# Eight routed experts on one core: turning the gathered tokens by DMA transposes of 16-bit planes instead of on TensorE

## The chip, the cores and the metric

One core of a Trainium2 chip. TensorE (PE) multiplies matrices and its results land in PSUM; VectorE (DVE), ScalarE (ACT) and GpSimd (POOL) work on vectors; SyncE (SP) only issues transfers here. Each engine runs its own list of instructions in order, and an instruction that waits holds up everything behind it on that engine. 16 DMA engines move data between the chip's memory (HBM) and the core's working memory (SBUF). The metric is the device time of one execution in microseconds (us).

## The reference

Attention with capped scores over 8 batches, 12 heads, 448 positions and a head dimension of 64 gives x, 3584 tokens of 768 numbers. Then a mixture of eight experts, where each expert gets exactly 448 tokens:

```python
logits = x @ w_gate                      # 3584 x 8
order = np.argsort(-logits.flatten())    # greedy, best first
for idx in order:
    tok, e = int(idx) // E, int(idx) % E
    if assigned[tok] >= 0 or counts[e] >= cap: continue   # cap = 448
    assigned[tok] = e; counts[e] += 1
for e in range(E):
    mask = assigned == e
    h = np.maximum(x[mask] @ w1[e], 0.0)   # 768 -> 1024
    out[mask] = h @ w2[e]                  # 1024 -> 768
```

All numbers are float32.

## The kernel before

**Attention** fills about the first 335 us and writes x to a DRAM tensor `xs`. It is the same in both kernels and is not needed further.

**Routing** (`Routing`). The order of assignment is found expert by expert: whichever expert fills up first is settled first, then its tokens are taken out and the next is searched. In this text the experts are numbered one to eight in that order (`p` is that number less one). A search finds a threshold by comparing a packed key of all tokens with several values at a time, over three key parts A, B, C: VectorE and ScalarE each take some of the comparisons (tiles `cmpD` and `cmpA`; each leaves a count in a column of `r_cd` or `r_ce`), then one small matmul on TensorE at line 507 adds the counts up and VectorE forms the next thresholds. `finalise`, the end of a routing, turns the threshold into a list of 448 token numbers: matmuls at lines 614, 615, 636 and 644, and last `idx`, the row numbers, on VectorE. The last expert needs no search (`last`).

**The experts** (`ffn_all`). Every float32 operand is split into a high part in TensorE's float32r form and a low remainder (`xgh`/`xgl`, `w1h`/`w1l`, `w2h`/`w2l`, two halves of `hh`), and a product is three matmuls. ScalarE makes the high parts (line 755 for weights) and GpSimd the low parts of the weights (line 759). The first layer (`ffn1`) takes 8 blocks of 18 matmuls, 128x128 by 128x448 at line 827; the second (`ffn2`) takes 8 blocks `u` of 24 or 16 matmuls, 128x128 by 128x384 at line 855. So an expert is 144 + 176 = 320 large matmuls, and this text calls them steps 1 to 320. Three PSUM buffers `psH` take the results in turn; ScalarE empties them (`hh`, `on`, `y`).

**What an expert needs first.** When the next expert's `idx` is there, GpSimd gathers its tokens from `xs` with four indirect DMAs (line 782) into the one tile `xg` (`xgp`), tokens on partitions. A matmul needs the 768 features on partitions, so x must be turned. `xtr(p,c)` does that for one chunk of 128 features: four TensorE transposes (line 798) into PSUM, then ScalarE writes `xgh` (line 803) and VectorE `xgl` (line 804). For expert two and later these chunks stand between the matmuls of the expert ahead.

**What sets the order.** Within `ffn_all` PE, ACT, DVE and POOL run in the order in which the program is written. `tick()` is called after each large matmul, counts steps in `now`, and resumes the routing, which is a generator: `yield n` asks to be resumed n steps later, and a negative number asks for an absolute step. So the routing's instructions lie between the large matmuls by step count, not by time. SP's order was left to the scheduler of the framework. The weights of the next expert are fetched by `load1` and `load2` on SP, once `ei`, the expert's number, is read (`TENSOR_LOAD ei`).

Of the kernel before, what the change touches and what calls it, by code (L numbers as in the profile page):

```python
# [7 lines left out]
AF=mybir.ActivationFunctionType; ALU=mybir.AluOpType; AX=mybir.AxisListType  # L8
# [323 lines left out]
class Routing:  # L332
# [266 lines left out]
    def finalise(s,wp,L,update):  # L599
# [49 lines left out]
        s.results.append((idx,s.ei))  # L649
        yield 1  # L650
        if update:
          with s.tc.issue_after(mark.ins) if s.cur==0 else nullcontext():
            z=wp.tile([112,1],F32,name="zz")
            v.tensor_scalar(z,oi[:,0,0,0:1],0.0,None,op0=ALU.mult)
# [14 lines left out]
    def phases0(s,wp,L,turned):  # L669
        HA=[7,10]; HB=3  # L670
        for p in range(s.E):
            s.hA=HA[min(p,len(HA))-1] if p else 7; s.hB=HB; s.na=2 if p<9 else 1
            s.cur=p
            if p:
                s.propose(L,0,s.NC)
                yield 30
            yield from (s.search(wp,turned if p==0 else ()) if p<s.E-1 else s.last(wp))
            yield -((p-1)*320+145) if p>1 else 4
            yield from s.finalise(wp,L,p<s.E-1)


W1B=4; W2B=4
def ffn_all(nc, tc, ctx, rt, xs, w1, w2, out, ident, E, wp, deferred, xctx, gen):
# [4 lines left out]
    res=rt.results  # L688
# [12 lines left out]
    ctx.enter_context(tc.manual_schedule(engines={ET.PE,ET.Activation,ET.DVE,ET.Pool}))  # L701
    with tc.issue_after(rt.mark[0].ins):
        units(1)
    posts()
    m=0
    wu=[None]; end=[-99]
# [64 lines left out]
    CP=[[int(y) if y!='-' else None for y in x] for x in ',,,,,-01,2-3,45'.split(',')]  # L771
# [5 lines left out]
    def gather(p):  # L777
        if p>=E or p in xgs: return
        need(p)
        t=xgs[p]=xgp  # L780
        for j,(o,n) in enumerate(TS):
            g=nc.gpsimd.indirect_dma_start(out=t[:n,j*DM:(j+1)*DM],out_offset=None,in_=xs,in_offset=bass.IndirectOffsetOnAxis(ap=res[p][0][:n,j:j+1],axis=0))  # L782
        return g
# [8 lines left out]
    def xtr(p,c):  # L792
        if p>=E or c is None: return
        newx(p)
        gather(p)
        ps=pt.tile([128,512],F32,name="psX")
        for j,(o,n) in enumerate(TS):
            nc.tensor.transpose(ps[:,o:o+128],xgs[p][:,j*DM+c*128:j*DM+c*128+128],ident)  # L798
        cutx(p,c,ps)
    def cutx(p,c,ps):  # L800
        h,l=xgT[p]
        src=ps[:,:C]
        nc.scalar.activation(h[:,c,:],src,AF.Copy)  # L803
        lo=nc.vector.tensor_tensor(l[:,c,:],src,h[:,c,:].bitcast(F32),op=ALU.subtract)
    pend=[]; cnt=[0]; cur=[0]; bc=[0]; BG=11
    def tick(n=1):
        cnt[0]+=n; bc[0]+=n; now[0]+=n
        if bc[0]>=BG:
            if pend: bc[0]=0; scatter(*pend.pop(0))
        if len(res)>cur[0]+1 and cur[0]+1 not in xgs: bc[0]=0; gather(cur[0]+1)  # L810
        if cnt[0]>=hint[0]:
            cnt[0]=0; step()
    hh={}
# [52 lines left out]
    need(0)  # L866
    WG=3; NW=12; WJ=4
    for i in range(WG): load1(0,i)
    mk=gather(0)
    with tc.issue_after(mk.ins):  # L870
        tok=xgp[0:1,2*DM:2*DM+1]
        for i in range(WG,W1B): load1(0,i,tok)
        load2(0,0,tok)
        load2(0,1,tok)
    warm(NW)
    step(); step()
    step()
# [5 lines left out]
    for p in range(E):  # L883
        lastp=p==E-1; cur[0]=p
        for f in range(FC):
            if f==0: load2(p,2)
            if f+W1B-1<FC and (p==0 or f+W1B-1>=W1B): load1(p,f+W1B-1) if (p,1,f+W1B-1) not in raw else None
            if f==2: load2(p,3)
            work={}
            if f+2<FC and (p,1,f+2) not in spl: work[3]=[lambda: split1(p,f+2)]  # L890
            at={0:[(11,0,0)],1:[(11,0,1)],2:[(11,0,2)],3:[(11,1,0)],4:[(11,0,3)],5:[(11,1,1)],6:[(11,1,2)],7:[(11,1,3)]}
            if p==0: at={1:[(11,0,0)],2:[(11,0,1)],3:[(11,0,2)],4:[(11,0,3)],5:[(11,1,0)],6:[(3,1,1),(11,1,2)],7:[(3,1,3)]}
            for n,hf,i in at.get(f,()): work[n]=[lambda hf=hf,i=i: split2(p,hf,i)]
            if p==1 and f==0: work[1]=[lambda: xtr(1,4)]; work[4]=[lambda: xtr(1,5)]
            ffn1(p,f,work)
        if lastp:
            while pend: scatter(*pend.pop(0))
            ih=f2.tile([128,2],I32,name="ih")
            for k in range(2): nc.gpsimd.tensor_scalar(ih[:,k:k+1],res[p][0][:,2:3],2.0,float(k),op0=ALU.mult,op1=ALU.add)
            nc.gpsimd.drain()  # L900
            lp[0]=False
            out2=out.rearrange("n (q d) -> (n q) d",q=2)
            for t,hf in [(t,hf) for t in (3,0,1,2) for hf in range(2)]:
                ffn2(p,t,hf,[])
                if t==2: put(out2,ih[:,hf:hf+1],ons[p][0][:,t*DM+hf*HD:t*DM+hf*HD+HD])
                elif hf==1: scatter(p,t)
            break
        for u in range(8):
            if u==4: load1(p+1,0); load1(p+1,1)
            if u==5: load1(p+1,2); load2(p+1,0)  # L910
            if u==6: load1(p+1,3)
            if u==7: load2(p+1,1)
            wk={5:{14:[lambda: split1(p+1,0)]},6:{8:[lambda: split1(p+1,1)]}}.get(u,{})
            if p<1 and u==7: wk={15:[lambda: xtr(1,3)]}
            ffn2(p,u%4,u//4,(CL if p<1 else CP)[u],wk)
            if u>3: pend.append((p,u%4))


def full(nc,tc,q,k,v,cap,wg,w1,w2,out):
    with ExitStack() as ctx:  # L920
# [2 lines left out]
        xs=dr.tile([3584,768],F32,name="xs")  # L923
        NDEF=4
        xd=dr.tile([2 if NDEF<4 else NDEF-2,128,6,448],F32,name="xd")
        ident=cp.tile([128,128],F32,name="ident"); make_identity(nc,ident)
        L1=cp.tile([112,32,8],F32,name="L1")
        r=Routing(nc,cp,3584,8); r.ident=ident; r.tc=tc
# [18 lines left out]
        ffn_all(nc,tc,ctx,r,xs,w1,w2,out,ident,8,wp,deferred,xctx,r.phases(wp,L1,turned))  # L947


_INS=["q","k","v","cap","moe_w_gate","moe_w1","moe_w2"]  # L950
# [24 lines left out]
```

## Time and profile before

| | |
|---|---|
| median of 3 runs | 906.47 us (906.41 to 906.98) |
| the profiled execution: its own time | 906.85 us |
| its span, first to last instruction | 905.1 us |
| granted TensorE clock, mean | 0.995 |
| ACT, DVE, POOL busy | 564.0, 604.0, 349.9 us |

The profiled execution is 1.75 us longer than its span (start and end of the program lie outside the span) and 0.38 us over the median. Busy times overlap between engines. PE's matmuls are pipelined, so the duration of one (0.34 or 0.36 us) is longer than its distance from the next; the distance between starts is what counts.

### The profile page before, as it was taken

How to read it: one execution, taken by the hardware profiler on the slowest of the kernel's cores; microseconds unless marked ns; L12 is line 12 of the kernel's file. 1: busy time of each engine (PE TensorE's matmuls, PEld its weight loads, DVE VectorE, ACT ScalarE, POOL GpSimd, SP SyncE). 2: the span in 40 equal slices, each digit the busy share in tenths (PEclk: the TensorE clock that was granted, in tenths of full speed). 3: DMA queues.
4: the chain of work that ended last, by engine and by line, in shares of the span. 5: the costliest groups of instructions: out<-in, count | busy, mean ns of one | idle time of the engine just before them, and what ended most of it. 6: DMA issues, size and time to landing. Idle time of an engine off the chain costs nothing.

```text
span 905.1 us, 17559 instructions
## 1 busy us (share of the span) xinstructions
PE 876.5 (97%) x6320; PEld 643.3 (71%) x6320; DVE 604.0 (67%) x2004; ACT 564.0 (62%) x844; POOL 349.9 (39%) x501
## 2 busy tenths in 40 slices
PE   6899999999999997799999999999999999999997
PEld 3333444444333345789989989989999999999997
DVE  3688988989888888766776776767767764231210
ACT  6998898889899948273582672762752752532521
POOL 8100000000000009482593492592682773754841
PEclk9999999999999999999999999999999999999999
DMA  8799999997994017741915616407407407416301
GB/s 117 113 136 140 128 171 173 139 164 120 198 175 72 1 58 246 248 157 45 313 45 171 196 36 226 157 19 236 150 18 253 149 3 251 149 55 236 112 10 53
DMA packets 291704, 123.09 MB, mean 136 GB/s; under 512 B 224768, under 2 KB 275712, under 8 KB 291104
## 3 DMA queue, kind: packets, MB, share of 16 engines
q1 hardware_dynamic: 285104, 99.70, 49.9%
q0 software_dynamic: 4656, 22.02, 6.8%
q8 instruction: 50, 0.82, 0.4%
q10 hardware_dynamic: 1856, 0.23, 0.2%
q14 instruction: 38, 0.31, 0.1%
HBM read 97.15 MB, written 24.77 MB: 135 GB/s over the span
## 4 chain that ended last, share of the span: by engine, by line
PE 72%; issue 12%; POOL 5%; DVE 5%; SPq 3%; DMA 1%; ACT 1%; POOLq 0%; ACTq 0%; DVEq 0%
PE psH L827 20%; PE psH L855 18%; PE psA L189 12%; PE psS L148 10%; PE psM L206 4%; SPq L92 2%; PE psS L153 2%; POOL w1l L759 2%; PE psX L798 2%; PE psM L37 1%; POOL out_dram L840 1%; POOL w2l L759 1%; DVE es L165 1%; POOL xg L782 1%; DVE cmpD L503 1%
## 5 line engine op out<-in xcount | busy, mean ns | idle before, releaser
L855 PE MATMUL psH<-w2h,hh 128*128 128x384 f32 x896 | 247.0, 342 | 0.0
L855 PE MATMUL psH<-w2l,hh 128*128 128x384 f32 x512 | 175.0, 342 | 0.0
L154 ACT ACTIVATE e<-psS 128x896 f32<-128x896 f32 x168 | 147.6, 909 | 31.3 <-PE psS L148 18.7
L855 PEld LDWEIGHTS psH<-w2h,hh 128*128 128x128 f32 x896 | 162.3, 189 | 0.2
L159 ACT ACTIVATE e<-e,bias 128x1792 f32<-128x1792 f32 (+2 forms) x74 | 147.3, 1991 | 2.0
L827 PE MATMUL psH<-xgh,w1h 128*128 128x448 f32 x384 | 143.4, 373 | 0.3 <-ACT xgh L803 0.3
L827 PE MATMUL psH<-xgh,w1l 128*128 128x448 f32 x384 | 141.6, 369 | 0.0
L827 PE MATMUL psH<-xgl,w1h 128*128 128x448 f32 x384 | 141.2, 368 | 0.0
L148 PE MATMUL psS<-tq,tk 64*64 64x448 f32 x1152 | 130.9, 548 | 7.4 <-DVE tq L133 3.4
L759 POOL TENSOR_TENSOR w1l<-w1r,w1h 128x768 fp32r<-128x768 f32 x62 | 114.2, 1843 | 28.6 <-ACT w1h L755 22.5
L189 PE MATMUL psA<-e,nv 64*64 64x448 f32 x1104 | 120.9, 541 | 1.2 <-DVE xT L199 1.2
L759 POOL TENSOR_TENSOR w2l<-w2r,w2h 128x768 fp32r<-128x768 f32 x64 | 118.1, 1846 | 9.0 <-ACT w2h L755 8.7
L459 POOL TENSOR_SCALAR r_Bt<-r_b 112x4 f16<-112x4 int32 x1 | 0.2, 199 | 303.7 <-DVE rin L243 303.7
L165 DVE TENSOR_TENSOR es<-es,e 64x896 f32<-64x896 f32 (+2 forms) x74 | 100.4, 1356 | 2.7 <-ACT e L159 1.3
L835 DVE SCALAR_TENSOR_TENSOR hh<-psH,hh 128x64 fp32r<-128x64 f32 (+1 forms) x128 | 44.1, 386 | 81.2 <-ACT hh L833 79.7
L861 ACT ACTIVATE on<-psH 128x384 f32<-128x384 f32 x48 | 23.6, 491 | 119.6 <-PE psH L855 119.6
L855 PEld LDWEIGHTS psH<-w2l,hh 128*128 128x128 f32 x512 | 96.5, 189 | 0.0
L148 PEld LDWEIGHTS psS<-tq,tk 64*64 64x64 f32 x1152 | 43.7, 133 | 73.9 <-issue 40.7
L189 PEld LDWEIGHTS psA<-e,nv 64*64 64x64 f32 x1104 | 46.5, 134 | 59.9 <-issue 50.5
L833 ACT ACTIVATE hh<-psH 128x448 fp32r<-128x448 f32 x64 | 34.8, 544 | 73.2 <-PE psH L827 61.1
L827 PEld LDWEIGHTS psH<-xgh,w1h 128*128 128x128 f32 x384 | 72.5, 189 | 5.9 <-ACT xgh L803 0.5
L827 PEld LDWEIGHTS psH<-xgh,w1l 128*128 128x128 f32 x384 | 72.3, 188 | 5.7
(334 smaller groups left out, 1320.6 us busy)
## 6 DMA issues: line engine op xcount, KB each, us to landing
w1r<-in_moe_w_dram SPq DMA_DIRECT2D x64, 384.0 KB, 3.9
w2r<-in_moe_w_dram SPq DMA_DIRECT2D x32, 768.0 KB, 8.0
k<-in_k_dram SPq DMA_DIRECT2D x92, 112.0 KB, 3.4
q<-in_q_dram SPq DMA_DIRECT2D x92, 112.0 KB, 4.0
nv<-in_v_dram SPq DMA_DIRECT2D x72, 128.0 KB, 3.9
xs<-xn SPq DMA_DIRECT2D x4, 1344.0 KB, 7.4
xs<-xn SPq DMA_DIRECT2D x4, 896.0 KB, 5.1
xd<-xT SPq DMA_DIRECT2D x2, 1344.0 KB, 7.0
```

Of the source, the lines that this page charges most:

```text
L148: for c in range(2): nc.tensor.matmul(ps[c*64:c*64+64,h,:S],tks[g,0][hp,o,u*128+c*64:u*128+c*64+64],tks[g,1][hp,o,:],start=True,stop=True)
L154: nc.scalar.activation(ev(g,r),ps[:,:,:S],AF.Tanh,scale=sr[0])
L159: act=lambda: nc.scalar.activation(e,e,AF.Exp,scale=sr[1],bias=bias)
L165: t=es_t[g]; add=lambda o,a,b: nc.vector.tensor_tensor(o,a,b,op=ALU.add)
L189: nc.tensor.matmul(avp[g,o][h*64:h*64+64,:S],lhs,rhs[hp,h,:],start=(j==0 and x==0),stop=j==3)
L206: nc.tensor.matmul(ps[g*32:g*32+32,:S],lhs,rhs,start=first,stop=last)
L759: (eng or nc.gpsimd).tensor_tensor(view(l),r,view(h).bitcast(F32),op=ALU.subtract)
L827: nc.tensor.matmul(ps[:,:C],a[:,c,:],b[:,c,:],start=(m==0),stop=(m==DC*3-1)); m+=1
L833: nc.scalar.activation(h[:,:C],ps[:,:C],AF.Relu)
L835: nc.vector.scalar_tensor_tensor(h[:,d:d+b-a],ps[:,a:b],0.0,h[:,a:b].bitcast(F32),op0=ALU.max,op1=ALU.subtract)
L855: nc.tensor.matmul(ps[:,:HD],h[:,f,a:a+128],spl[p,2,hf,f//2][w][:,f%2,:],start=(m==0),stop=(m==nm-1))
L861: if t<3: nc.scalar.activation(ons[p][0][:,t*DM+hf*HD:t*DM+hf*HD+HD],ps[:,:HD],AF.Copy)
```

## The change

1. For experts three to eight the TensorE transposes are gone. Instead, for each of the four gathered groups of tokens (128, 128, 128 and 64 rows), ScalarE copies the tile `xg` as 16-bit numbers into a tile `pl`, low halves and high halves apart (the "planes"; 1536 numbers per row, two buffers), and SP writes `pl` to a DRAM tensor `xz`. When all four are written, two DMA transposes on SP, 384 columns each, bring `xz` back turned, into the same tile `xg`, where the halves meet again as float32. Then `cutt` splits two chunks at a time (ScalarE 128x896, VectorE 128x896), at three places in block 6 of the second layer.
2. The four plane copies are placed 22, 30, 38 and 46 steps after the gather. Two of the next expert's first-layer weight loads are asked for right at the gather.
3. The end of a routing from expert three on may start at step 100 of the expert ahead (before: 145). Where the search ends later than that, it starts 4 steps after the search. So the 614/615/636/644 matmuls and the gather lie earlier.
4. SP is now also in written order. Two ordering hints around the start of the experts are dropped.

```diff
-            yield -((p-1)*320+145) if p>1 else 4
+            yield -((p-1)*320+100) if p>1 else 4
...
+    TD=22; TJ=8; xq=[]
+    def planes(p,j):
+        o,n=TS[j]
+        pl=fp.tile([128,2,DM],I16,name="pl",bufs=2)
+        nc.scalar.activation(pl[:n],xgs[p][:n,j*DM:(j+1)*DM].bitcast(I16).rearrange("p (d h) -> p h d",h=2),AF.Copy)
+        nc.sync.dma_start(xz[2*o:2*o+2*n].rearrange("(p h) d -> p h d",h=2),pl[:n])
+        if j==3:
+            for a in (0,3): nc.sync.dma_start_transpose(xgp[:,a*C:a*C+3*C].bitcast(I16).rearrange("p (c t) -> p c t",c=3),xz[:,a*128:a*128+384])
+    def cutt(p,c0,c1):
+        newx(p)
+        h,l=xgT[p]
+        x=xgp[:,c0*C:c1*C].rearrange("p (c t) -> p c t",c=c1-c0)
+        nc.scalar.activation(h[:,c0:c1,:],x,AF.Copy)
+        nc.vector.tensor_tensor(l[:,c0:c1,:],x,h[:,c0:c1,:].bitcast(F32),op=ALU.subtract)
...
-        if len(res)>cur[0]+1 and cur[0]+1 not in xgs: bc[0]=0; gather(cur[0]+1)
+        if len(res)>cur[0]+1 and cur[0]+1 not in xgs:
+            bc[0]=0; n=cur[0]+1; gather(n)
+            if n>1:
+                load1(n,0); load1(n,1)
+                xq.extend((now[0]+TD+TJ*j,lambda j=j: planes(n,j)) for j in range(4))
+        while xq and xq[0][0]<=now[0]: xq.pop(0)[1]()
...
-            if u==4: load1(p+1,0); load1(p+1,1)
+            if u==4 and p<1: load1(p+1,0); load1(p+1,1)
...
-            ffn2(p,u%4,u//4,(CL if p<1 else CP)[u],wk)
+            if p and not lastp:
+                for m,c in {6:[(4,0),(12,2),(20,4)]}.get(u,()): wk[m]=wk.get(m,[])+[lambda c=c: cutt(p+1,c,c+2)]
+            ffn2(p,u%4,u//4,CL[u] if p<1 else [],wk)
```

The order on **ScalarE** in the second layer of expert four, while expert five is made ready, before. `hh` is the last result of the first layer, `on` and `y` empty the second layer's PSUM blocks, `cmpA` are the comparisons of the search for expert six:

```order
L833 ACTIVATE hh<-psH 128x448
L861 ACTIVATE on<-psH 128x384 x3
L500 ACTIVATE cmpA,r_cd_315<-r_VAt,r_T8A 128x252
L864 ACTIVATE y_8359<-psH 64x384
L500 ACTIVATE cmpA,r_ce_307<-r_VAt,r_H8A 128x252 x2
L861 ACTIVATE on<-psH 128x384
```

And after:

```order
L850 ACTIVATE hh<-psH 128x448
L802 ACTIVATE pl<-xg 128x1536
L878 ACTIVATE on<-psH 128x384
L802 ACTIVATE pl<-xg 128x1536 x2
L500 ACTIVATE cmpA,r_cd_316<-r_VAt,r_T8A 128x252
L802 ACTIVATE pl<-xg 64x1536
L878 ACTIVATE on<-psH 128x384
L500 ACTIVATE cmpA,r_ce_308<-r_VAt,r_H8A 128x252 x2
```

The four plane copies now stand between the PSUM blocks, and the first comparison of the next search stands behind the third of them. In the program the first copy waits for the first gather, the second for the second, the third for the third gather and for the write of the first copy's buffer to `xz`, the fourth for the last gather and the second write.

The order on **SP** from the reading of the next expert's number on, at the same place, before (`ISA` and `TENSOR_LOAD` set the address):

```order
L734 TENSOR_LOAD ei
L734 ISA x2
L743 ISA
L743 DMA w1r<-in_moe_w_dram 128x6x128
L743 ISA
L743 DMA w1r<-in_moe_w_dram 128x6x128
L743 ISA
L743 DMA w1r<-in_moe_w_dram 128x6x128
L750 ISA
L750 DMA w2r<-in_moe_w_dram 128x2x768
```

And after:

```order
L733 TENSOR_LOAD ei
L733 ISA x2
L742 ISA
L742 DMA w1r<-in_moe_w_dram 128x6x128
L742 ISA
L742 DMA w1r<-in_moe_w_dram 128x6x128
L803 DMA xz<-pl 128x1536 x3
L803 DMA xz<-pl 64x1536
L805 DMA_TRANSPOSE xg<-xz 128x3x896 x2
L742 ISA
L742 DMA w1r<-in_moe_w_dram 128x6x128
L749 ISA
```

Six rows are put in; the loads behind them keep their order, but are now queued behind the writes and the transposes, which wait for ScalarE and for the writes to land.

The order on **PE** around the last matmul of expert five's routing (line 644), before, in the second layer:

```order
L855 MATMUL psH<-w2h,hh 128x384 x2
L855 MATMUL psH<-w2l,hh 128x384
L644 LDWEIGHTS r_sel
L644 MATMUL psR<-ev,r_sel 128x28
L855 MATMUL psH<-w2h,hh 128x384 x2
```

And after, in the first layer:

```order
L844 MATMUL psH<-xgl,w1h 128x448
L844 MATMUL psH<-xgh,w1l 128x448
L644 LDWEIGHTS r_sel
L644 MATMUL psR<-ev,r_sel 128x28
L844 MATMUL psH<-xgh,w1h 128x448
```

Counted in steps, this matmul moves from behind step 183 to behind step 138 of expert four; for experts six, seven and eight likewise. For expert four it moves from 183 to 152, because its search ends later, and for expert three it stays at 188. The first line-507 matmul of the following search stands 55 steps behind the line-644 matmul in both kernels.

More of the change, by code (lines that the diff above doesn't have):

```diff
@@ L651, in finalise @@
         if update:
-          with s.tc.issue_after(mark.ins) if s.cur==0 else nullcontext():
+          if True:
             z=wp.tile([112,1],F32,name="zz")
@@ L677, in phases0, with ffn_all @@
             yield from (s.search(wp,turned if p==0 else ()) if p<s.E-1 else s.last(wp))
-            yield -((p-1)*320+145) if p>1 else 4
+            yield -((p-1)*320+100) if p>1 else 4
             yield from s.finalise(wp,L,p<s.E-1)
 W1B=4; W2B=4
-def ffn_all(nc, tc, ctx, rt, xs, w1, w2, out, ident, E, wp, deferred, xctx, gen):
+def ffn_all(nc, tc, ctx, rt, xs, xz, w1, w2, out, ident, E, wp, deferred, xctx, gen):
     C=448; DM=768; DC=6; DF=1024; FC=8; HD=384
@@ L700, in ffn_all @@
     N0=1; UN=[1,2,1,2,0,2,2,1,2,2,0,2,2,2,0,0]
-    ctx.enter_context(tc.manual_schedule(engines={ET.PE,ET.Activation,ET.DVE,ET.Pool}))
-    with tc.issue_after(rt.mark[0].ins):
-        units(1)
+    ctx.enter_context(tc.manual_schedule(engines={ET.PE,ET.Activation,ET.DVE,ET.Pool,ET.SP}))
+    units(1)
     posts()
@@ L770, in ffn_all @@
     xgs={}; xgT={}
-    CP=[[int(y) if y!='-' else None for y in x] for x in ',,,,,-01,2-3,45'.split(',')]
     CL=[[]]*6+[[None,None,0],[1,2]]
@@ L868, in ffn_all @@
     for i in range(WG): load1(0,i)
[L869 to L874, printed above, removed]
+    gather(0)
+    tok=xgp[0:1,2*DM:2*DM+1]
+    for i in range(WG,W1B): load1(0,i,tok)
+    load2(0,0,tok)
+    load2(0,1,tok)
     warm(NW)
@@ L925, in full @@
         xd=dr.tile([2 if NDEF<4 else NDEF-2,128,6,448],F32,name="xd")
+        xz=dr.tile([896,768],I16,name="xz")
         ident=cp.tile([128,128],F32,name="ident"); make_identity(nc,ident)
@@ L946, in full @@
         deferred=[lambda f=f: f((px,xr)) for f in deferred]
-        ffn_all(nc,tc,ctx,r,xs,w1,w2,out,ident,8,wp,deferred,xctx,r.phases(wp,L1,turned))
+        ffn_all(nc,tc,ctx,r,xs,xz,w1,w2,out,ident,8,wp,deferred,xctx,r.phases(wp,L1,turned))
 _INS=["q","k","v","cap","moe_w_gate","moe_w1","moe_w2"]
```

## The prediction

> **What bounds the kernel now.** The page first, then busy time by stretches over one whole expert (first layer of expert four, then its second layer).
>
> ```profile
> span 905.1 us, 17559 instructions
> PE 876.5 (97%) x6320; PEld 643.3 (71%) x6320; DVE 604.0 (67%) x2004; ACT 564.0 (62%) x844; POOL 349.9 (39%) x501
> ...
> 581.96:611.60 29.64, 29.64 (x150) 26.45 (x151) 20.59 (x104) 20.09 (x42) 26.84 (x29) 1.00 0.16 46
> 611.60:647.31 35.71, 35.71 (x223) 33.92 (x223) 26.16 (x123) 14.78 (x38) 11.32 (x12) 1.00 0.65 217
> ```
>
> PE is busy all of both stretches (35.71 of 35.71 us), at full clock. So each matmul taken out of the second layer shortens the time by its distance to the next, and each wait put in front of PE lengthens it. ScalarE is busy for only 14.78 of the 35.71 us there: room in sum, but it runs in order.
>
> The timeline of PE gives the distances.
>
> ```profile
> 621.24 0.51 PE L855 MATMUL psH<-w2h,hh 128*128 128x384 f32 x2
> ...
> 624.88 0.34 PE L855 MATMUL psH<-w2h,hh 128*128 128x384 f32 x1
> ...
> 631.81 0.34 PE L855 MATMUL psH<-w2h,hh 128*128 128x384 f32 x1
> 631.99 0.18 PE L507 MATMUL psR<-r_ce,r_bo 128*128 128x8 bf16 x1
> ...
> 632.29 0.33 PE L855 MATMUL psH<-w2l,hh 128*128 128x384 f32 x1
> ...
> 636.54 0.60 PE L798 MATMUL psX<-ident,xg 128*128 128x128 f32 x4
> 636.89 0.42 PE L855 MATMUL psH<-w2l,hh 128*128 128x384 f32 x1
> 637.15 0.52 PE L855 MATMUL psH<-w2h,hh 128*128 128x384 f32 x2
> L798 PE MATMUL psX<-ident,xg 128*128 128x128 f32 x176 | 26.4, 272 | 0.0
> ```
>
> From 621.24 to 624.88 lie 21 steps (seven triples): 0.173 us a step. A line-507 matmul makes two steps last 0.48 instead of 0.35: 0.13 us for a small matmul, somewhat less where several stand together.
>
> **The gain.** Four transposes take 636.54 to 636.89, 0.35 us, and the step behind them lasts 0.26 instead of 0.173: together 0.44 us a chunk. The group has 176 transposes, 44 chunks; two belong to expert one and six to expert two and stay. 36 x 0.44 = **15.9 us** go. ScalarE's and VectorE's splits of PSUM chunks go with them, but those waited for PE and not PE for them.
>
> **What is put in, and who waits.** Time T counts from the start of the second layer of the expert ahead (611.60 in the rows).
>
> ```profile
> 609.53 1.85 POOL L759 TENSOR_TENSOR w2l<-w2r,w2h 128x768 fp32r<-128x768 f32 x1 [1.03 <-ACT w2h L755]
> 619.02 0.19 PE L644 MATMUL psR<-ev,r_sel 128*128 128x28 f16 x1
> 619.93 0.98 POOL L782 DMA_INDIRECT xg<-xs,idx  x1 [8.55 <-DVE zz L654]
> 624.07 1.13 POOL L782 DMA_INDIRECT xg<-xs,idx  x1 [0.30 <-issue]
> 626.10 0.27 PE L477 MATMUL psR<-r_id,r_VA 112*128 112x112 f16 x2
> 626.90 0.51 ACT L500 ACTIVATE cmpA<-r_VAt,r_T8A 128x252 bf16<-128x252 f16 x1 [1.33 <-DVE r_VAt L482]
> 627.31 0.19 ACT L500 ACTIVATION_READ_ACCUMULATOR cmpA<-r_VAt,r_T8A 128x1 bf16 x1
> 628.90 0.18 PE L507 MATMUL psR<-r_cd,r_bo 128*128 128x4 bf16 x1
> ```
>
> This is the end of expert five's routing and the start of expert six's search. The first of four gathers starts 0.9 us behind the line-644 matmul, the fourth 4.1 us later. ScalarE's first comparison ran 626.90 to 627.50, 1.4 us ahead of the line-507 matmul that needs it. In the changed order that comparison stands behind the third plane copy, so three durations decide:
>
> ```profile
> DMA to landing us min/median/max: 4.4/8.0/9.2
> ...
> 614.71 1.63 SPq L743 DMA_DIRECT2D w1r<-in_moe_w_dram  x3
> 616.53 0.73 SPq L750 DMA_DIRECT2D w2r<-in_moe_w_dram  x1
> 617.51 0.37 SPq L743 DMA_DIRECT2D w1r<-in_moe_w_dram  x1
> ...
> L755 ACT ACTIVATE w1h<-w1r 128x768 fp32r<-128x768 f32 x64 | 53.5, 836 | 9.4 <-DMA w1r<-in_moe_w_dram 9.4
> L159 ACT ACTIVATE e<-e,bias 128x1792 f32<-128x1792 f32 x48 | 85.9, 1790 | 1.2
> L861 ACT ACTIVATE on<-psH 128x384 f32<-128x384 f32 x48 | 23.6, 491 | 119.6 <-PE psH L855 119.6
> ...
> w1r<-in_moe_w_dram SPq DMA_DIRECT2D x64, 384.0 KB, 3.9
> xs<-xn SPq DMA_DIRECT2D x4, 448.0 KB, 4.3
> out_dram<-on,ih POOLq DMA_INDIRECT x2, 2.6
> ```
>
> - Gather: the first row is the landing of `xg`. The median 8.0 belongs to gathers that share the engines with the loads issued just ahead of them (rows at 614.71 to 617.51). In the new SP order only two `w1r` loads lie ahead, issued as soon as `ei` is known, some 6 us ahead of the gather, and everything else is behind the writes. I take 4.4, the least; the other end is 8.0.
> - Plane copy, 1536 numbers a row: no such row. Between 0.84 (768 numbers, if 16-bit numbers went twice as fast) and 1.8 (1792). On the line through these two rows 1.5; I take that, having no reason for a faster one.
> - Write of 384 KB to `xz`: between 2.6 (the smallest indirect write) and 4.3 (448 KB to DRAM on SP). The latter is nearest in size and direction; I take 4.0.
>
> Expert five (and six alike): line 644 stands 6 first-layer steps (29.64/144 = 0.206 each) ahead of the layer's end, T = -1.2; the gather could start at -0.3, and GpSimd is done with its last weight part at 611.38, T = -0.2. First tokens 4.2; copy until 5.7; its buffer is written to DRAM by 9.7; only then the third copy, until 11.2; comparison until 11.8. PE reaches its line-507 matmul behind step 193: 49 x 0.173 plus 0.2 for the line-477 pair = 8.7. PE runs in order, so the whole second layer stands behind that matmul. **PE waits 3.1 us**, twice 6.2.
>
> Expert four, line 644 behind step 152: T = 1.8; gather 2.7, tokens 7.1, copy 8.6, write 12.6, copy 14.1, one `on` (0.5) 14.6, comparison 15.2, against step 207 at 63 x 0.173 + 0.7 for small matmuls = 11.6: **3.6**. Expert three, steps 188 and 243: 8.4, gather 9.3, tokens 13.7, 15.2, 19.2, 20.7, `y` 21.2, comparison 21.8, against 99 x 0.173 + 1.1 = 18.3: **3.5**. Experts seven and eight: no search follows, no comparison stands between the copies; the PSUM block `u`=1 is emptied at about 14, and PE needs its buffer at the start of `u`=4 (T = 15.3). **0**.
>
> The transposes: no row shows one. They move 2 x 0.69 MB as rows of 256 bytes. The nearest rows, small packets in attention (45 to 90 us), weight loads at full pace (611 to 650 us), and the smallest transfer:
>
> ```profile
> DMA packets 41729, 6.22 MB, mean 138 GB/s; under 512 B 41722, under 2 KB 41722, under 8 KB 41722
> ...
> GB/s 0 0 0 0 18 202 310 311 266 273 390 371 343 395 391 426 369 400 400 221 246 117 22 0 183 221 0 0 0 138 387 282 0 120 329 383 346 334 91 126
> ...
> wgs<-in_moe_w_gate_dram SPq DMA_DIRECT2D x6, 4.0 KB, 2.0
> ```
>
> 41729 packets in 45 us are 927 a us; one transpose has 896 x 3 = 2688 packets: 2.9 us. At 390 GB/s it is 1.8, at 138 GB/s 5.0. I take 2.9, in the packet size the nearest, and 2.0 fixed: the second lands 7.8 us behind the issue. [...]
>
> Expert five: fourth copy behind the comparison, 13.3; its write lands 17.3; second transpose 25.1; `cutt` reads it at step 292, T = 25.6 + 1.1 + 3.1 = 29.8. Covered, with 4.7 us to spare; expert four has 20.7 + 7.8 = 28.5 against 30.5. Expert three is late: fourth copy 23.3, written 27.3, second transpose 35.1, second `cutt` 36.1 (896 numbers, 0.95 on the line of the two ScalarE rows), two comparisons 37.3, against the line-507 matmul behind step 308 at 164 x 0.173 + 1.9 + 3.5 = 33.8: **3.5 more**. Its queued weight loads (384 KB and 768 KB at 390 GB/s, 3 us) then land by about 39 and are first split behind step 3 of the next expert, T above 39: just covered.
>
> Moving the end of the routing costs PE nothing by itself: the same small matmuls at 0.13. VectorE has 9 us free in the first layer (20.59 of 29.64). SP's order is otherwise the same, and the dropped hints only swap four transposes around a wait at 335 us.
>
> **Sum.** -15.9 + 6.2 + 3.6 + 3.5 + 3.5 = +0.9 us. Against the profiled execution (906.85 = span 905.1 + 1.75) 907.8; that run lies 0.4 over the median, so **907** beside 906.47: no change that can be told, since about 0.2%, 1.8 us, is what a measurement of this kernel can tell.
>
> **Rivals.** (1) *Short waits, faster.* The write lands like the smallest indirect one (2.6) or the copy runs at 0.84: with both, expert five's comparison ends at 9.1 and the waits are 0.4 + 0.4 + 0.9 + 0.8 + 0.5 = 3.0, so 894; with only one of them 899 to 902. For it: ScalarE's idle time; against: a 16-bit `cmpA` of 252 numbers takes 0.51 us, no faster than 384 float32 numbers (0.49). Waits of nothing (890.6) need the third copy to start 0.9 us behind the first; no transfer in the rows lands within that.
> (2) *Slow transposes, slower.* At 138 GB/s the second lands 12 us behind its issue; expert three loses 4.2 more and four 2.2: 914. It decides from 9.8 us on in expert four, 12.5 in five and six.
> (3) *Late gathers, slower.* If they land in 8.0 as now, every one of four waits grows by 3.6: 922. Against it: the loads that crowd them are queued behind.
> (4) *Transposes at one engine's pace.* 400 GB/s over 16 engines is 25 GB/s; 1.38 MB take 55 us, some 45 us late in each of six experts: about 1180. For it nothing but that no row shows a transpose. [...]
>
> **How the numbers follow.** The forecast, 903.5 to 911 (each write or gather 0.5 us off moves the sum by 2 to 2.5): 0.48. Rival 1: 0.25. Rival 2, with paces between: 0.13. Rival 3: 0.09. Rival 4: 0.05. Of the forecast a quarter is below 904.7, half within 0.2%, a quarter above: faster 0.25 + 0.12 = 0.37, same 0.24, slower 0.39. The range leaves out the fastest part of rival 1 and rival 4 with the worst of 2 and 3: 897 to 922.
>
> **What would show it.** Right: no line-798 group beyond 32 transposes; PE waits of about 3 us at line 507, put down to ScalarE's `cmpA` or to a DMA, once in each of experts two to five, behind steps 243, 207, 193, 193; ScalarE idle ahead of the third `pl` for `xz`; period of experts seven's and eight's preparation about 62.7 instead of 65.35 us. Wrong: no such waits (rival 1), ScalarE idle ahead of `xgh` in every expert (2, 4), ahead of the first `pl` for more than 5 us (3).

## The result, and the profile after

The changed kernel takes 947.52 us (median of 4 runs, 944.04 to 948.64) beside 906.44 for the kernel before on the same chip: ratio 1.0449 [1.0418, 1.0481], 41 us slower. Predicted were 907, range 897 to 922. One execution of the third-buffer kernel below (1221 us at a clock of 0.65) and one of the kernel before (4509 us) were disturbed and are left out.

The page, of the execution that took 944.04 us:

```profile
span 942.2 us, 17356 instructions
PE 875.3 (93%) x6176; PEld 642.3 (68%) x6176; DVE 640.8 (68%) x1986; ACT 592.6 (63%) x850; POOL 348.4 (37%) x501
```

PE does 144 matmuls fewer and is busy hardly less (875.3 beside 876.5 us) in a span that is 37.1 us longer. VectorE, with 18 instructions fewer, is busy 36.8 us longer (640.8 beside 604.0): some of its instructions must have become longer.

Where the time lies, layer by layer, from PE's timeline (first large matmul of a layer to the first of the next, us):

| layer | before | after | difference |
|---|---|---|---|
| two, second | 35.36 | 40.43 | +5.07 |
| three, first | 30.29 | 33.32 | +3.03 |
| three, second | 35.09 | 35.26 | +0.17 |
| four, first | 30.24 | 36.93 | +6.69 |
| four, second | 35.11 | 37.05 | +1.94 |
| five, first | 30.25 | 38.33 | +8.08 |
| five, second | 35.10 | 39.57 | +4.47 |
| six, first | 30.25 | 38.60 | +8.35 |
| six, second | 34.02 | 30.53 | -3.49 |
| seven, first | 29.75 | 36.96 | +7.21 |
| seven, second | 34.03 | 30.53 | -3.50 |

The second layers together give +4.7, beside the forecast of +0.9. The first layers, for which the forecast was nothing, give **+33.4**.

Busy time by stretches of the kernel after: first and second layer of expert four, then of expert five.

```profile
589.32:626.25 36.93, 32.61 (x160) 28.55 (x159) 27.89 (x106) 19.32 (x38) 27.57 (x32) 0.95 0.36 115
626.25:663.30 37.05, 32.36 (x191) 30.71 (x190) 28.36 (x138) 22.01 (x47) 10.48 (x12) 1.00 0.81 251
663.30:701.63 38.33, 33.45 (x158) 29.36 (x158) 29.91 (x87) 17.59 (x32) 27.05 (x30) 0.91 0.22 67
701.63:741.20 39.57, 33.93 (x191) 32.27 (x190) 28.27 (x138) 22.00 (x47) 10.98 (x12) 0.96 0.79 239
```

The second number is PE's busy time, the seventh (behind GpSimd's, the fifth engine) the granted clock. In expert five's first layer PE is idle for 38.33 - 33.45 = 4.9 us, and busy for 33.45 us with work that took 30.25 before: the clock was 0.91. So the loss has two parts, a wait and slower matmuls behind it. Over the five first layers the waits are 19.7 us, and PE is busy 13.7 us longer: some 2 of these are the small matmuls that moved in (2.1 us in the run without low parts, below), the rest is the slower clock.

What PE waited for from 440 us on (in us: total, number, longest; the kernel before has no wait there):

```profile
PE psR L507 <- DVE cmpD L503: 11.6, 5, 2.9
PE psH L844 <- DVE hh L852: 9.8, 2, 4.9
PE psR L614 <- DVE ei L609: 8.7, 3, 4.2
PE psR L507 <- ACT cmpA L500: 6.8, 3, 2.7
```

The two middle rows, 18.5 us, belong to the first layers. Lines 609 and 852 are short VectorE operations; what stood ahead of them? VectorE in expert five's first layer, and GpSimd at the same time:

```profile
676.47 13.18 DVE L589 SCALAR_TENSOR_TENSOR qq<-r_K,wA,r_K 112x32 f32<-112x32 f32 x1
689.58 0.15 DVE L570 TENSOR_TENSOR wt<-psR,wm 112x8 f32<-112x8 f32 x1
...
690.12 1.28 DVE L852 SCALAR_TENSOR_TENSOR hh<-psH,hh 128x64 fp32r<-128x64 f32 x4
```

```profile
675.01 1.83 POOL L758 TENSOR_TENSOR w2l<-w2r,w2h 128x768 fp32r<-128x768 f32 x1
676.79 0.09 POOL L756 MEMSET gap<- 1x1 f32 x1
676.85 1.84 POOL L758 TENSOR_TENSOR w1l<-w1r,w1h 128x768 fp32r<-128x768 f32 x1
...
687.81 1.79 POOL L758 TENSOR_TENSOR w2l<-w2r,w2h 128x768 fp32r<-128x768 f32 x1
689.55 0.09 POOL L756 MEMSET gap<- 1x1 f32 x1
```

An operation on 112x32 numbers, 0.24 us where GpSimd is idle, lasts 13.18 us: it ends when GpSimd's row of low parts (line 758, back to back, with a 1x1 memset `gap` between) ends at 689.6. Queued behind it on VectorE is `hh`, which reads the PSUM buffers for the low halves. So it isn't ScalarE alone that empties them, as the description of the kernel has it, and PE runs out of buffers.

In expert four's first layer it is the end of the routing itself, each operation held for about one low part (1.8 us):

```profile
611.82 1.93 DVE L604 TENSOR_SCALAR gteq<-qq,wB 112x32 f16<-112x32 f32 x1
...
615.60 1.85 DVE L607 TENSOR_TENSOR_SCAN scan<-r_ones,gteq 112x64 f16<-112x64 f16 x1
```

In the kernel before, these operations took 0.23 to 0.29 us, after GpSimd's last low part of the layer.

And PE behind the wait: its timeline, then two stretches, during the wait and behind it.

```profile
690.95 0.71 PE L844 MATMUL psH<-xgh,w1h 128*128 128x448 f32 x1 [4.88 <-DVE hh L852]
691.45 0.57 PE L844 MATMUL psH<-xgl,w1h 128*128 128x448 f32 x1
691.83 0.57 PE L844 MATMUL psH<-xgh,w1l 128*128 128x448 f32 x1
...
696.61 0.37 PE L844 MATMUL psH<-xgh,w1l 128*128 128x448 f32 x1
```

```profile
686.00:691.00 5.00, 0.12 (x2) 0.09 (x1) 4.93 (x9) 1.27 (x2) 3.64 (x6) 0.88 0.00 0
691.00:694.40 3.40, 3.40 (x11) 2.94 (x12) 3.18 (x15) 0.00 (x0) 0.00 (x0) 0.50 0.05 12
```

After 4.88 us of waiting the matmuls start 0.37 us apart instead of 0.20, for 5.6 us, at a granted clock of 0.50. That is some 2.5 us on top of the wait. The last section shows how idle TensorE was ahead of each fall of the clock.

### The profile page after: what moved, and what is told of

The parts are those of the page before. It is cut to its first block, busy times and chain, and to the rows that moved or that the text cites. A ratio compares the mean times of both kernels' runs of the same rounds, so it can differ in the third digit from the quotient of the medians.

```text
span 942.2 us, 17356 instructions
## 1 busy us (share of the span) xinstructions
PE 875.3 (93%) x6176; PEld 642.3 (68%) x6176; DVE 640.8 (68%) x1986; ACT 592.6 (63%) x850; POOL 348.4 (37%) x501
## 4 chain that ended last, share of the span: by engine, by line
PE 27%; issue 14%; DVE 7%; POOL 5%; DMA 4%; ACT 3%; POOLq 0%; SPq 0%; ACTq 0%
PE psH L844 16%; PE psH L872 10%; DVE qq L589 3%; POOL w1l L758 2%; DMA xz<-pl 2%; POOL out_dram L857 1%; DMA xg<-xs,idx 1%; POOL w2l L758 1%; POOL xg L780 1%; DVE xgl L811 1%; ACT cmpA L500 1%; DVE cmpD L503 1%; ACT xgh L810 1%; DMA xg<-xz 1%; ACT pl L802 1%
## 5 line engine op out<-in xcount | busy, mean ns | idle before, releaser
L154 ACT ACTIVATE e<-psS 128x896 f32<-128x896 f32 x168 | 147.4, 909 | 31.2 <-PE psS L148 18.5
L872 PEld LDWEIGHTS psH<-w2h,hh 128*128 128x128 f32 x896 | 165.0, 191 | 0.2
L844 PE MATMUL psH<-xgh,w1h 128*128 128x448 f32 x384 | 147.8, 385 | 10.1 <-DVE hh L852 9.8
L844 PE MATMUL psH<-xgl,w1h 128*128 128x448 f32 x384 | 146.1, 381 | 0.0
L844 PE MATMUL psH<-xgh,w1l 128*128 128x448 f32 x384 | 144.7, 377 | 0.0
L148 PEld LDWEIGHTS psS<-tq,tk 64*64 64x64 f32 x1152 | 43.8, 132 | 73.2 <-issue 37.1
L857 POOL DMA_INDIRECT out_dram<-on,idx x31 | 30.9, 997 | 163.1 <-ACT on L878 120.5
L844 PEld LDWEIGHTS psH<-xgh,w1h 128*128 128x128 f32 x384 | 75.5, 197 | 16.6 <-issue 10.4
L844 PEld LDWEIGHTS psH<-xgl,w1h 128*128 128x128 f32 x384 | 75.6, 197 | 5.3
```

The source lines that it names most:

```text
L148: for c in range(2): nc.tensor.matmul(ps[c*64:c*64+64,h,:S],tks[g,0][hp,o,u*128+c*64:u*128+c*64+64],tks[g,1][hp,o,:],start=True,stop=True)
L154: nc.scalar.activation(ev(g,r),ps[:,:,:S],AF.Tanh,scale=sr[0])
L844: nc.tensor.matmul(ps[:,:C],a[:,c,:],b[:,c,:],start=(m==0),stop=(m==DC*3-1)); m+=1
L857: st=nc.gpsimd.indirect_dma_start(out=dst,out_offset=bass.IndirectOffsetOnAxis(ap=ix,axis=0),in_=src,in_offset=None)
L872: nc.tensor.matmul(ps[:,:HD],h[:,f,a:a+128],spl[p,2,hf,f//2][w][:,f%2,:],start=(m==0),stop=(m==nm-1))
```

## The experiments

**Theory A**: the end of the routing, moved into the first layer, meets GpSimd's low parts on VectorE. **Theory B**: the planes, their writes and the transposes cost it, in the first layer through late loads. **Theory C**: the routing's end is too long for the first layer anyway.

### The two halves of the change alone

Transposes alone, the changed kernel with

```diff
-            yield -((p-1)*320+100) if p>1 else 4
+            yield -((p-1)*320+145) if p>1 else 4
```

> The changed kernel with the end of the routing put back to step 145; only the turning by DMA transposes is left. Theory A (routing end in the first layer collides with GpSimd): in the changed kernel the first layers of experts three to seven lost 3.0, 6.7, 8.1, 8.4 and 7.2 us, 33.4 in all, against 4.7 for the second layers; here the first layers are back at about 30.3 us, and the second layers of experts two to five lose about 5 each like expert two's in the changed kernel, since all tokens now come as late as expert three's; about 906.5 + 20 - 7 = 920, range 912 to 926. Theory B (the plane copies, writes and transposes are what costs, also in the first layer, by late weight loads that leave GpSimd with a backlog): first layers stay long and the time is 940 or more.

The move alone, the kernel before with

```diff
-            yield -((p-1)*320+145) if p>1 else 4
+            yield -((p-1)*320+100) if p>1 else 4
```

> The kernel before with only the number 145 changed to 100. Theory A: the VectorE operations of lines 589, 603 to 607 and 618 wait for GpSimd's low parts here too, with TensorE turning as before: first layers of experts three to seven lose most of the 33.4 us, time 925 to 942, and line 589 or 603 show single durations of 5 us or more. Theory B: 905 to 909, durations of 0.25 to 1.9 us.

Measured: transposes alone 927.76 us, ratio 1.021 [1.0165, 1.0254]; the move alone 935.03, ratio 1.0314 [1.0297, 1.0331]. One number, with nothing else changed, costs 28.8 us. Its two longest waits on PE, and the stretch of expert four's first layer:

```profile
PE psH L827 <- DVE hh L835: 10.1, 2, 5.1
PE psR L614 <- DVE ei L609: 8.2, 3, 3.7
```

```profile
583.12:619.90 36.78, 33.47 (x160) 29.43 (x159) 26.82 (x97) 18.23 (x35) 27.09 (x30) 0.91 0.35 107
```

First layers of experts three to seven are 32.52, 36.78, 38.05, 37.36 and 36.49: 30.4 us more than before, against 33.4 in the changed kernel. The second layers are unchanged or up to 0.8 us shorter, by the small matmuls that left them. Theory B is out as the main cause of the first layers, but not as a cause of anything there. With the transposes alone the first layers of three to seven are 30.3, 31.3, 33.7, 32.0 and 32.4, 9 us more than before and 24 less than in the changed kernel; the total is 8 us above what I expected of theory A (and 2 above the range), which is about these 9. In the trace they are waits of 6.5 us, mostly for comparisons queued behind `y` and for `xgh` and `xgl`, and some slow clock (0.95 in expert five's first layer); no run took them apart. The two halves together (50 us) are more than the change (41): with the early routing end the tokens come earlier, and the second layers of two to five are 5 us shorter in all than with the transposes alone.

### GpSimd out of the way

The move alone, with no low parts from expert three on:

```diff
-        (eng or nc.gpsimd).tensor_tensor(view(l),r,view(h).bitcast(F32),op=ALU.subtract)
+        if key[0]<2 or name not in cz: (eng or nc.gpsimd).tensor_tensor(view(l),r,view(h).bitcast(F32),op=ALU.subtract)
+        if key[0]>1: cz[name]=l
```

> The kernel before with 145 changed to 100, and GpSimd's low parts of the weights left out from expert three on (its matmuls read one fixed low tile instead, so the numbers are not the reference's; PE does the same matmuls). Theory A (VectorE's end of the routing waits for GpSimd's low parts): with GpSimd idle in the first layers the 30 us that the move alone cost are gone, first layers at 30.3 us, total 902 to 907, and no operation of lines 589 to 618 over 0.3 us. Theory C (the end of the routing is too long for its 38 steps of the first layer in any case, or PE's small matmuls cost it): 925 to 936 as with the move alone.

Measured: 906.43 us beside 906.23, ratio 0.9999 [0.999, 1.0009] (10 runs). The groups of lines 589 and 603, of the move alone and then of this kernel (the last columns: busy us, mean ns of one, idle time ahead):

```profile
L589 DVE SCALAR_TENSOR_TENSOR qq<-r_K,wA,r_K 112x32 f32<-112x32 f32 x5 | 28.7, 5730 | 0.0
L603 DVE TENSOR_SCALAR gt<-qq,wB 112x32 f32<-112x32 f32 x6 | 8.3, 1382 | 0.0
```

```profile
L603 DVE TENSOR_SCALAR gt<-qq,wB 112x32 f32<-112x32 f32 x6 | 1.4, 234 | 0.0
L589 DVE SCALAR_TENSOR_TENSOR qq<-r_K,wA,r_K 112x32 f32<-112x32 f32 x5 | 1.2, 243 | 0.0
```

Same instructions, same order on VectorE and PE; without GpSimd's low parts `qq` falls from 5730 to 243 ns, the first layers of three to seven are 29.9 to 30.8, and all of the 28.8 us are gone. Theory A is shown, and theory C is out: 38 steps of the first layer are enough when GpSimd is idle.

### Which operation is held

In the changed kernel, one of the two tiles that `qq` adds is first copied to PSUM:

```diff
-        else: mid=[lambda: row(keep[0],tB)]
+        else:
+            k2=s.vps[:112,448:448+s.NC]
+            mid=[lambda: row(keep[0],tB),lambda: nc.scalar.activation(k2,s.T["K2"],AF.Copy)]
...
-            s.best(wp,0,s.pw[:112,0:8]); s.pw=s.pw[:112,8:16]
+            s.best(wp,0,s.pw[:112,0:8],k2); s.pw=s.pw[:112,8:16]
```

> The changed kernel, but K2, one of the two tiles that line 589 (qq) adds, is first copied by ScalarE into PSUM, so that VectorE reads only one operand from SBUF there. If it is the two SBUF operands that must wait for GpSimd (Theory A), qq takes 0.25 us each time instead of 13.2 twice, and experts five and six get back their 8.1 and 8.4 us of first layer: 944 - 16 = 928, range 925 to 934. If qq's 13 us are a wait for data or for VectorE's queue that the profile puts on it, nothing changes: 940 to 948.

And the changed kernel with a second memset between GpSimd's low parts:

```diff
-            if tt[0]: nc.gpsimd.memset(gap,0.0)
+            if tt[0]: nc.gpsimd.memset(gap,0.0); nc.gpsimd.memset(gap,0.0)
```

> The changed kernel with two of the 1x1 memsets (gap) instead of one ahead of each of GpSimd's low parts. Theory A, if the VectorE operation gets in only when GpSimd pauses long enough: qq (line 589) and gt (line 603) get in at the next pause, at most 1.9 us each, and some 20 us of the first layers' 33 come back: 918 to 930. Theory B or a wait of another kind: no gain, 943 to 950, since GpSimd's first layer gets 1.3 us longer.

Measured: 943.0 (940.04 to 948.0) and 948.4 us (946.65 to 950.95), beside 947.52: 4.5 us at most from the first (ratio 1.0414 [1.0374, 1.0454], an interval that overlaps the changed kernel's), nothing from the second (1.0473 [1.0449, 1.0496]), where theory A expected 16 us from the first and some 20 from the second. Yet each did to `qq` what was expected. K2 in PSUM, then two gaps (groups and one row on VectorE, waits on PE):

```profile
L591 DVE SCALAR_TENSOR_TENSOR qq<-r_K,wA,psV 112x32 f32<-112x32 f32 x5 | 1.2, 237 | 0.0
756.42 12.64 DVE L577 SCALAR_TENSOR_TENSOR sx<-wt,wB,r_e8c 112x8 f32<-112x8 f32 x1
PE psR L616 <- DVE ei L611: 11.5, 4, 4.2
```

```profile
L589 DVE SCALAR_TENSOR_TENSOR qq<-r_K,wA,r_K 112x32 f32<-112x32 f32 x5 | 5.9, 1183 | 0.0
L630 DVE TENSOR_TENSOR oh<-r_ihi,hi 112x512 f16<-112x512 int16 x6 | 8.9, 1484 | 0.0
PE psR L636 <- DVE oi L632: 18.5, 4, 4.8
```

With K2 in PSUM `qq` takes 237 ns, and in expert six's routing end the 13 us pass to `sx`, a few operations on, with both inputs in SBUF; in expert five's, `sx` and lines 606, 607 and 609 are held for about one low part each (1.67 to 1.92 us). With two gaps `qq` takes 1.2 us, but the operations behind it lose up to one low part each, as far as `oh`, eleven behind `gt` (2.02 us instead of 0.42); PE waits 18.5 us there. So no single operation is the cost: a dozen of them follow one another in the end of the routing, and a row of low parts of 1.8 us each stands against all of them. The wait is set by when GpSimd's row ends, and helping one operation hands it to the next.

### The waits of the second layer

From here on all kernels have the transposes and, unless another step is named, step 145. A third place for the planes, so that the third copy need not wait for the first write:

```diff
-        pl=fp.tile([128,2,DM],I16,name="pl",bufs=2)
+        if j==2: pl=ws.tile([128,DC,128],F32,name="w1r",bufs=W1B).rearrange("p c f -> p (c f)").bitcast(I16).rearrange("p (h d) -> p h d",h=2)
+        else: pl=fp.tile([128,2,DM],I16,name="pl",bufs=2)
```

> The changed kernel with the routing end at 145 and a third buffer for the planes (a slot of the weight tiles), so that the third plane copy no longer waits for the first write to xz. My working put 4.0 us of every wait at line 507 on that write; the profile shows 3.1 to 3.6 from the end of the copy to the landing. In four experts each wait at line 507 falls from about 3 to 0 or 0.5, and the clock that falls behind each wait stays up: 928 - 4 x 4 = 912, range 906 to 918. If the waits are VectorE's own (cmpD late) or the gathers', no gain: 924 to 930.

The same at step 128:

> The third buffer with the routing end at step 128 instead of 145: VectorE begins it some 26 us into the first layer, when GpSimd is nearly done with its low parts. Theory A: first layers lose at most 2 us each, and the tokens come about 3 us earlier, so the second transposes land sooner: 2 to 8 us below the same kernel at 145. If GpSimd is still busy then: slower than that kernel by up to 10.

And with the third and fourth copy on GpSimd, the splits later:

```diff
+        if j<2: nc.scalar.activation(pl[:n],src,AF.Copy)
+        else: nc.gpsimd.tensor_copy(pl[:n],src)
...
-                for m,c in {6:[(4,0),(12,2),(20,4)]}.get(u,()): wk[m]=wk.get(m,[])+[lambda c=c: cutt(p+1,c,c+2)]
+                for m,c in {6:[(16,0)],7:[(4,2),(12,4)]}.get(u,()): wk[m]=wk.get(m,[])+[lambda c=c: cutt(p+1,c,c+2)]
```

> As the third buffer, and the third and fourth plane copies are made by GpSimd instead of ScalarE, the splits of the turned tokens placed later (steps 296, 308, 316). ScalarE's comparison then stands behind two copies only: no wait at line 507 behind a copy in any expert. If ScalarE's order was all that cost in the second layer: 928 - 22 = 905 or below, down to 892 where the transposes stay covered. GpSimd's copy of 1536 16-bit numbers has no row; at 2 to 4 us the transposes land up to 5 us later than with ScalarE, and then the waits move to the splits of the turned tokens: 905 to 920.

Measured, beside 927.76: third buffer 919.53 us, ratio 1.015 [1.0129, 1.0172]; at step 128 914.91, 1.0084 [1.0058, 1.011]; two planes on GpSimd 911.03, 1.0056 [1.0039, 1.0073]. The layers are those of the profiled executions, of 906.85, 929.26, 917.32 and 906.84 us; the last is the fastest of its kernel's ten.

| layer | before | transposes alone | third buffer | two planes on GpSimd |
|---|---|---|---|---|
| two, second | 35.36 | 42.39 | 41.53 | 32.74 |
| three, first | 30.29 | 30.26 | 30.40 | 35.60 |
| three, second | 35.09 | 40.03 | 36.02 | 32.42 |
| four, first | 30.24 | 31.28 | 31.28 | 34.05 |
| four, second | 35.11 | 37.70 | 36.04 | 32.41 |
| five, first | 30.25 | 33.75 | 32.00 | 33.23 |
| five, second | 35.10 | 37.48 | 36.53 | 32.41 |

The third buffer took 7.5 us out of four second layers, half of what I expected, and the total is 1.5 above its range: PE now waits there mainly for VectorE's comparisons `cmpD` (0.7 to 3.1 us each). With only two copies on ScalarE the second layers are 2.6 to 2.7 us shorter than before: this is the gain of the prediction, 15.9/6 = 2.65 a layer, bare of waits. It isn't one edit, since the splits moved too, and the loss is now in the first layers. On ScalarE, SP and GpSimd at expert two's second layer:

```profile
508.38 0.95 ACT L813 ACTIVATE xgh<-xg 128x896 fp32r<-128x896 f32 x1 [0.32 <-DMA xg<-xz]
512.92 0.95 ACT L813 ACTIVATE xgh<-xg 128x896 fp32r<-128x896 f32 x1 [3.20 <-DMA xg<-xz]
```

```profile
502.08 6.70 SPq L808 DMA_TRANSPOSE xg<-xz  x2
```

```profile
496.38 1.46 POOL L805 COPY w1r<-xg 128x1536 int16<-128x1536 int16 x1 [2.77 <-DMA xg<-xs,idx]
```

GpSimd copies as fast as ScalarE (1.46 beside 1.48 us). The second transpose lands 10.8 us behind the issue of the first, after expert three has begun (511.69). At step 128 the first layers of four to seven are 32.6 to 32.8, 2.4 to 3.1 above those before (0.6 to 1.4 above the same kernel at 145), and PE waits 6.2 us for `ei` in five places (2.7 the longest): step 128 is still too early, by theory A, though the earlier tokens outweigh it there.

### Towards a faster version

Two planes on GpSimd, with only the places of the splits moved ({6:[(20,0)],7:[(12,2),(15,4)]}):

> As two planes on GpSimd, only the splits of the turned tokens placed differently (steps 300, 316, 319 instead of 296, 308, 316), so that ScalarE doesn't stand at the second transpose ahead of a comparison. If the 2.5 us wait at line 507 behind step 312 came from the comparison queued behind that split, it goes and TensorE waits only at the first steps of the next first layer, 1 us or less: 898 to 906. If the transposes' landing decides alone, 906 to 914.

And with the transposes divided by tokens:

```diff
-            for a in (0,3): nc.sync.dma_start_transpose(xgp[:,a*C:a*C+3*C].bitcast(I16).rearrange("p (c t) -> p c t",c=3),xz[:,a*128:a*128+384])
+            for a,(b,e) in enumerate(((0,512),(512,896))): nc.sync.dma_start_transpose(xgp[:,:DC*C].bitcast(I16).rearrange("p (c t) -> p c t",c=DC)[:,:,b:e],xz[a])
...
+                for m,c in {7:[(2,0),(8,2),(14,4)]}.get(u,()): wk[m]=wk.get(m,[])+[lambda c=c: cutt(p+1,c,c+2)]
```

> As two planes on GpSimd, but the two DMA transposes divide the tokens instead of the features: one brings the first 256 tokens (ready some 3 us earlier), one the last 192, and the splits of the turned tokens all stand in the last block (steps 306, 312, 318). There the second transpose landed 10.8 us behind the issue of the first, 0.4 us after expert three's first layer began, and waits of 0.3 to 2.5 us and the slower clock behind them made the first layers 2 to 5 us longer. If the end of the second transpose comes 3 us earlier, these go: first layers at 31 to 32, second at 32.4, 906.8 - 5 x 2.5 = 894, range 888 to 903. If rows of the transposes cost by their number, which here doubles the columns for each, no gain: 905 to 915.

On top of that, the products with `xgl` last in the first block, and then step 140 and earlier splits as well:

```diff
+        if p>1 and f==0: seq=[(c,k) for c in range(DC) for k in (0,2)]+[(c,1) for c in range(DC)]
```

> As rows apart, and in the first block of each first layer from expert three on the six matmuls with xgl stand last instead of each second in its triple. TensorE waited 3.4 us in six places for xgl there (0.7 at most each) and 1.6 for xgh; if that and the slower clock behind it are what is left of the loss in the first layers (32.2 beside 30.3 us), they fall to 30.5 to 31.3: 903.3 - 5 = 898, range 895 to 902. If they come from the comparisons queued behind the splits (line 507), no change: 901 to 905.

> The same, with the routing end at step 140 and the splits of the turned tokens two steps earlier (304, 310, 316). GpSimd's last low part of a first layer is issued at step 137, so the first VectorE operations of the routing end meet it at most once. If tokens 1 us earlier matter more than that: 1 to 4 us below low x last. Theory A in the small: where GpSimd is still busy at step 140, one operation waits up to 1.85 us and the time is 1 to 5 us above it.

| kernel | us | ratio to before |
|---|---|---|
| splits moved | 908.33 | 1.0032 [1.0019, 1.0046] |
| transposes by tokens | 903.29 | 0.9986 [0.9966, 1.0006] |
| and `xgl` last | **901.83** | **0.9964 [0.9952, 0.9977]** |
| and step 140 | 902.88 | 0.9974 [0.9962, 0.9985] |

With the splits moved alone, expert three's first layer fell from 35.60 to 33.60, but those of four to six stayed at 33.3 to 33.7, and the time lies in the range of the second reading, by which the landing decides. Dividing by tokens came out 0.3 above its range's upper end, and its interval takes in no change; `xgl` last is faster than the kernel before by 4 us, 0.4%. Its time lies in the ranges of both readings, and the first layers of four to six decide for the second: they stayed at 32.2 to 32.3 us, as the waits moved from `xgl` to the comparisons of line 507. What it has over the transposes by tokens, 1.5 us, is less than the spread of either. Step 140 is 1.0 above it, with first layers of 32.8 instead of 32.2 to 32.3; the intervals overlap. What PE still waits for with `xgl` last:

```profile
PE psR L507 <- DVE cmpD L503: 5.2, 3, 1.7
PE psH L848 <- ACT xgh L813: 4.2, 2, 2.4
```

These first layers are still 2 us over the 30.25 of before (expert three's, at 34.5, is 4 over). On VectorE, at the start of expert four's (the next comparisons stand behind this row, and PE's line-507 matmul waits 1.7 us for it):

```profile
579.62 3.09 DVE L814 TENSOR_TENSOR xgl<-xg,xgh 128x896 fp32r<-128x896 f32 x3 [0.48 <-ACT xgh L813]
```

Moving this was not tried.

## Why the prediction was wrong

**The step that failed** is "Moving the end of the routing costs PE nothing by itself ... VectorE has 9 us free in the first layer (20.59 of 29.64)". The runs put 30.4 us of first layers and 28.8 us of time on that move alone, and 0.2 us on it when GpSimd is idle. VectorE's 9 us were free, but most of the layer belonged to GpSimd, whose 26.84 busy us of 29.64 stood in the same quoted row: operations of the routing's end, like `qq`, got through only where it paused (13.18 us instead of 0.24). None of my rivals named GpSimd. The profile of before held a warning that I did not quote (durations: least, median, most, in ns):

```profile
L589 DVE SCALAR_TENSOR_TENSOR qq<-r_K,wA,r_K x6: 243/834/842, 422.8 to 736.5; 112x32 f32<-112x32 f32 x6
L575 DVE SCALAR_TENSOR_TENSOR sx<-wt,wB,r_e8c x7: 226/1506/1511, 364.3 to 737.7; 112x8 f32<-112x8 f32 x7
```

The same instruction on the same shape takes 0.24 or 0.84, 0.23 or 1.51 us. The long ones are those that meet a low part.

**A term that was missing**: PE's slower clock behind a wait. I priced waits by their length alone; some 11 us of the first layers came on top (the 13.7 without the small matmuls that moved in), and some 4 us of the second: those of experts two and five hold 35.2 and 33.9 us of busy PE, where two planes on GpSimd needs 32.7 and 32.4 in all.

**The gain** of 15.9, 2.65 a layer, was right: 2.6 to 2.7 in the second layers of two to five with nothing in the way. In those of experts six and seven the changed kernel got 3.5, since 0.8 of small matmuls left them with the move.

**The waits of the second layer**: forecast 3.5 + 3.5 (three), 3.6 (four), 3.1 and 3.1 (five, six), 16.8 in all; measured idle 5.2, 2.8, 4.7 and 5.6, 18.4 in all. The first of them in expert five's preparation, ScalarE and then PE:

```profile
629.76 1.49 ACT L802 ACTIVATE pl<-xg 128x1536 int16<-128x1536 int16 x1 [2.77 <-DMA xg<-xs,idx]
...
634.90 1.48 ACT L802 ACTIVATE pl<-xg 128x1536 int16<-128x1536 int16 x1 [1.61 <-DMA xz<-pl]
636.29 0.49 ACT L500 ACTIVATE cmpA<-r_VAt,r_T8A 128x252 bf16<-128x252 f16 x1
```

```profile
636.92 0.17 PE L507 MATMUL psR<-r_cd,r_bo 128*128 128x4 bf16 x1 [1.80 <-ACT cmpA L500]
660.75 0.18 PE L507 MATMUL psR<-r_ce,r_bo 128*128 128x8 bf16 x1 [2.89 <-DVE cmpD L503]
```

The third copy waits for the write, the comparison stands behind it, and PE waits 1.80 instead of 3.1 us. The terms: copy 1.49 (1.5 predicted), write from the end of the first copy (631.25) to its landing (634.90) 3.65 (4.0), gather 5.1 in the median (4.4). The second row of TensorE is a wait that I did not have, 2.9 us in experts five and six each: `xgl` stands ahead of the comparisons there:

```profile
655.10 1.09 DVE L811 TENSOR_TENSOR xgl<-xg,xgh 128x896 fp32r<-128x896 f32 x1 [0.74 <-ACT xgh L810]
...
656.68 2.18 DVE L811 TENSOR_TENSOR xgl<-xg,xgh 128x896 fp32r<-128x896 f32 x1
```

The second takes twice the first; GpSimd had a low part from 655.89 to 657.9. I followed ScalarE's half of `cutt` and not VectorE's. This reading is from the trace; no run took it apart. So that the second layers came out near the forecast is in part luck: -15.9 of transposes, -1.8 of small matmuls that left (as in the move alone), +18.4 of waits, of which 5.8 were not among mine, and +4 of slower clock make the +4.7.

**The transposes**: for expert three the second landed 8.8 us behind the issue (7.8 predicted), and PE waited 2.9 and 2.3 us (3.5 and 3.5). Rival 4 is out; for experts four and later they were covered, as forecast, as long as the tokens came early.

## What to carry to other kernels

Before moving small VectorE operations into a stretch with "free" VectorE time, look at what GpSimd does there: here, where it ran back to back on SBUF in low parts of 1.8 us, operations of 0.23 to 0.29 us lasted 1.85 to 1.93 us each (expert four), and `qq` 13.18 us, until GpSimd's row ended (expert five). Look for the same instruction at several durations (0.24, 0.83, 13.2 us): it shows the collision before it is the bound. Price a wait of TensorE that the clock falls behind at its length plus what it cost here, 1.6 to 2.8 us: after it the first layer's matmuls ran 0.37 us apart instead of 0.20 for 3.4 to 6.2 us.

## What the runs showed of the hardware

- A VectorE operation with both inputs in SBUF lost to GpSimd many times in a row: `qq` sat through seven whole low parts and the seven 1x1 memsets ahead of them (13.18 us, in experts five and six alike); with two memsets its mean is 1.18 us, with one input in PSUM 0.24, without low parts 0.24. In experts three and four of the same run, and in four places of the kernel before, it got in at the first memset (0.83 to 0.84 us); what decides that stays open. The low part under way when expert five's `qq` began ended 0.37 us later; why `qq` sat through seven more is not shown.
- Whether the clock falls behind a wait can't be read from its length alone. In the changed kernel it fell behind waits of 2.33 and 2.75 us and behind one of 2.88 (501.71), and stayed at 1.00 behind two of 2.89 (660.75 and 738.65). In the trace of the changed kernel the changes of the granted clock lie on a grid of 3.41 us (to 0.002 us, between 370 us and the last 8 us), and the clock of a cell of that grid went with TensorE's idle share of the cell before (by the busy times of the profile). From 440 us on, all 7 cells at full clock that were idle for 61% or more were followed by half clock and none of the other 128 was, of which the idlest had 52%; no cell lay between. In the kernel before, none of the 134 cells had idle time and the clock stayed at 1.00. From half clock it came back behind all 7 cells without idle time and behind none of the 3 with 17% to 35%. In the changed kernel, the wait that ended at 713.26 fills most of one cell, and the clock falls in the next; of the 2.89 us that ended at 660.75, the cell below holds only the last 1.71:

```profile
710.24:713.65 3.41, 0.66 (x8) 0.49 (x7) 0.17 (x2) 2.42 (x4) 0.00 (x0) 1.00 0.15 59
713.65:717.06 3.41, 3.41 (x12) 3.41 (x12) 2.07 (x12) 2.39 (x6) 0.00 (x0) 0.50 0.54 163
659.04:662.45 3.41, 1.70 (x11) 1.71 (x12) 3.34 (x15) 0.14 (x2) 1.07 (x2) 1.00 1.08 332
662.45:665.86 3.41, 3.41 (x19) 3.05 (x18) 2.83 (x18) 2.55 (x7) 1.01 (x3) 1.00 0.81 316
```

- Two DMA transposes, 1.38 MB together, took SP 5.7 to 6.7 us to issue in the changed kernel (six pairs), and for expert three's pair 6.70 with two planes on GpSimd, 7.82 divided by tokens and 6.97 with `xgl` last. In the changed kernel each pair moved as 5376 packets of 256 bytes. Expert three's second landed 8.8 us behind the first issue there and 10.8 with two planes on GpSimd.
